# Chunk-selected attention with a gated projection: half-batch units for all heads, one fp32 transpose of keys and queries, and scores of a head pair in row tiles

## Chip, cores, metric

The kernel runs on one core of one Trainium2 chip. The metric is the device time of one execution in microseconds. Each kernel was run several times and compared with runs of the kernel before on the same chip.

## The reference, cut to what matters

Four batches, 8 heads, 768 positions, head size 64. Keys fall into 24 chunks of 32. For each query and chunk an upper bound of the score is computed from the chunk's minimum and maximum; each query keeps its six best chunks, and causal attention runs over those. The result (3072 rows of 512) goes through a gated projection with inner size 1536.

```python
k_min, k_max = k_chunks.min(axis=3), k_chunks.max(axis=3)        # 24 chunks of 32 keys
ub = sum over d of max(q * k_min, q * k_max)                     # bound per query and chunk
top_chunks = argsort(where(causal_chunk, ub, -1e9))[..., -6:]
scores = q @ k.T / 8, masked to the chosen chunks and to j <= i
attn = softmax(scores); x = attn @ v                             # (4, 768, 8*64)
out = (sigmoid(x @ w_gate) * (x @ w_val)) @ w_out                # 3072 x 512
```

## The kernel before

Work goes in 8 groups, each four heads of one batch over all 768 positions. The keys and queries of a head are turned so that head size lies on the partitions, in fp16, 64 rows; under them lie 32 more rows, which for the keys hold a fixed pattern (minus 60000 at the positions of chunk c in row c) and for the queries hold 1 where chunk c was *not* chosen. One matmul with 96 rows then gives score plus mask.

```python
def chunk_bounds(g):                       # kc: a second copy of the keys, one chunk per partition
    kv = d["kc"].rearrange("p s d -> p d s")
    nc.vector.tensor_reduce(kmm[:, 0:64], kv, AX.X, ALU.max)
    nc.vector.tensor_reduce(kmm[:, 64:128], kv, AX.X, ALU.min, negate=True)
...
def score(g, h, x):
    hk, hq = headK[4 * (g % 2) + h], headQ[4 * (g % 2) + h]      # both [96, 768]
    ...
    for (jb, i0, w) in banks[x]:
        nc.tensor.matmul(ps[:, o:o + w], hk[:, 128 * jb:128 * jb + 128], hq[:, i0:i0 + w],
                         start=True, stop=True)
        o += w
    nc.scalar.activation(at[:, b0:b0 + n], ps, AF.Exp, scale=scale)
...
for g in range(NG):                        # the projections of batch b run beside batch b + 1
    if g % 2 == 0 and g > 0:
        ffn = ffn_tasks(g // 2 - 1)
```

The chunk bounds are fp32 matmuls that write 32 output partitions each, so the four heads of a group use four column strips of the array at once. The projections of one batch (`ffn_gv`, `ffn_out`) are interleaved with the attention of the next batch.

The softmax here doesn't subtract the row's maximum and nothing guards it: scores larger than these inputs give would overflow.

## Time and profile before

| | before |
|---|---|
| time, median (4 runs) | 394.27 us |
| span of the profiled run | 393.6 us |
| TensorE matmul busy | 320.2 us (81%) |
| VectorE / ScalarE / GpSimd busy | 230.0 / 204.6 / 73.5 us |
| projections, third gate block starts | 114.1 us |
| TensorE idle between matmuls, whole span | 61.4 us |

From the page of the kernel before come busy time, the slices (each digit is the busy tenth of one fortieth of the span, 9 is 90% or more), and the granted TensorE clock in tenths (9 is full here, 5 is half):

```profile
span 393.6 us, 6906 instructions
...
PE 320.2 (81%) x2696; PEld 197.2 (50%) x2696; DVE 230.0 (58%) x486; ACT 204.6 (52%) x393; POOL 73.5 (19%) x77
...
PE   1071549287598999799979998799999999999996
...
PEclk9996557856969999999999999999999999999999
DMA  9999999297920964433615010002000100100102
```

The first quarter differs from the rest: TensorE is idle for nearly half of it (54 of 114 us in the table below) and often at half clock, while the DMA engines are full for most of it. After slice 12 TensorE hardly rests. The table of windows of the kernel before says the same in numbers (length of the window, busy time and instruction count of each engine, granted clock, DMA share, GB/s):

```profile
core 0: us, PE busy (x) PEld busy (x) DVE busy (x) ACT busy (x) POOL busy (x), PEclk, DMA share, GB/s
0.00:114.00 114.00, 59.58 (x509) 39.52 (x510) 77.07 (x156) 49.78 (x90) 36.34 (x43) 0.76 1.02 185
190.00:231.00 41.00, 36.95 (x337) 22.84 (x336) 27.52 (x57) 25.24 (x49) 7.88 (x7) 1.00 0.32 78
```

In the first quarter the chain of waits of the kernel before (start, length, what) goes through loads and the chunk reductions, not through TensorE:

```profile
0.81 5.91 DMA kc_151<-in_k_dram
6.74 3.59 DVE kmm_209 L140
10.33 3.50 DVE kmm_209 L141
...
39.69 11.32 DMA k_177<-in_k_dram
51.16 1.35 POOL k_1_349 L132
```

This is the timeline of TensorE in the kernel before around the chunk bounds (start, length, engine, line, operation, operands):

```profile
210.28 0.32 PE L287 MATMUL v_0_7_2464<-xT_1_1617,wv_146 128*128 128x384 f16 x1
210.44 0.33 PE L287 MATMUL v_0_7_2464<-xT_2_2033,wv_146 128*128 128x384 f16 x1
210.60 0.33 PE L287 MATMUL v_0_7_2464<-xT_3_2194,wv_146 128*128 128x384 f16 x1
210.86 0.46 PE L169 MATMUL ubT_2446<-qcat_0_2281,kcat_142 128*32 128x320 f32 x1
...
211.71 0.43 PE L169 MATMUL ubT_2446<-qcat_3_2386,kcat_142 128*32 128x320 f32 x1
212.07 0.34 PE L281 MATMUL g_0_8_2471<-xT_0_1456,wg_145 128*128 128x384 f16 x1
```

A matmul's length in the record (0.33 us for 384 columns) is not what it costs in a dense stream; that is the step to the next start, here 0.16 us (0.42 ns per column). Between the last full-array matmul (210.60) and the first one on a 32-column strip (210.86) the step is 0.26: 0.1 us more than streaming. On the way back it is 0.36 us where the passes among themselves step by 0.27.

### The profile page before, as it was taken

What the parts mean: (1) busy time and instruction counts of PE and PEld (TensorE: products, weight loads), DVE (VectorE), ACT (ScalarE), POOL (GpSimd) and SP (SyncE); (2) the same over time, 40 slices, a digit from 0 to 9 for tenths busy, and PEclk for the clock granted to TensorE, in tenths of its full rate; (3) what the DMA queues carried; (4) which work ended last, traced back from release to release, by engine and by line L of the source; (5) the groups of instructions that cost most, each with busy time, mean ns of one, the idle gap of its engine ahead of it and who ended that gap; (6) DMA issues with size and microseconds to landing.
All of it is one profiled execution on the core that took longest, in us unless ns stands there. A gap on an engine that the chain in (4) does not pass through costs nothing.

```text
span 393.6 us, 6906 instructions
## 1 busy us (share of the span) xinstructions
PE 320.2 (81%) x2696; PEld 197.2 (50%) x2696; DVE 230.0 (58%) x486; ACT 204.6 (52%) x393; POOL 73.5 (19%) x77
## 2 busy tenths in 40 slices
PE   1071549287598999799979998799999999999996
PEld 0040335164464656455645555465666566565552
DVE  4947629967949745855596658664556544142230
ACT  1150446266576548555556656655876466332331
POOL 4504143232312051003300230011101001000000
PEclk9996557856969999999999999999999999999999
DMA  9999999297920964433615010002000100100102
GB/s 181 217 214 214 208 212 195 66 217 148 214 62 15 226 156 108 101 62 86 155 42 120 28 55 0 2 2 80 2 2 27 55 2 1 55 27 28 54 2 80
DMA packets 84400, 36.62 MB, mean 93 GB/s; under 512 B 75920, under 2 KB 80528, under 8 KB 83600
## 3 DMA queue, kind: packets, MB, share of 16 engines
q1 hardware_dynamic: 79616, 31.47, 37.3%
q0 software_dynamic: 4752, 4.72, 7.2%
q8 instruction: 21, 0.34, 0.4%
q14 instruction: 11, 0.09, 0.1%
HBM read 34.60 MB, written 6.29 MB: 104 GB/s over the span
## 4 chain that ended last, share of the span: by engine, by line
PE 58%; DVE 17%; ACT 8%; issue 6%; SPq 5%; DMA 4%; POOL 1%; ACTq 0%; DVEq 0%; POOLq 0%
SPq L125 5%; DMA k_177<-in_k_dram 3%; DMA kc_151<-in_k_dram 2%; DVE kmm_1096 L140 1%; DVE kmm_209 L140 1%; DVE kmm_721 L141 1%; DVE kmm_1096 L141 1%; DVE kmm_209 L141 1%; PE o_0_0_2626 L296 1%; PE o_0_0_3781 L296 1%; PE o_384_0_3203 L296 1%; PE o_384_0_2048 L296 1%; PE o_0_0_1471 L296 1%; PE o_384_2_4783 L296 1%; PE o_384_1_4298 L296 1%
## 5 line engine op out<-in xcount | busy, mean ns | idle before, releaser
L287 PEld LDWEIGHTS <-wv_146 128*128 128x128 f16 x384 | 37.9, 99 | 28.3 <-issue 4.2
L281 PEld LDWEIGHTS <-wg_145 128*128 128x128 f16 x384 | 35.7, 99 | 23.2 <-issue 6.7
L153 PE MATMUL qT_0_212<-ident_103,q_148 128*128 128x128 f32 x5 | 1.3, 426 | 8.4 <-DMA q_148<-in_q_dram 8.4
L243 PEld LDWEIGHTS <-hk_123 96*128 96x128 f16 x48 | 4.8, 122 | 3.8 <-issue 2.9
L153 PE MATMUL qT_1_227<-ident_103,q_148 128*128 128x128 f32 x5 | 1.3, 427 | 5.9 <-DVE qcat_1_221 L160 5.9
L153 PE MATMUL qT_0_369<-ident_103,q_176 128*128 128x128 f32 x5 | 1.3, 426 | 5.8 <-DMA q_176<-in_q_dram 5.8
L140 DVE TENSOR_REDUCE kmm_1096<-kc_1044 96x64 f32<-96x2048 f32 x1 | 3.7, 3667 | 3.7 <-PE kct_756 L146 3.7
L272 PE MATMUL xps_1_671<-ident_108,xnat_400 128*128 128x128 f16 x6 | 0.8, 307 | 6.1 <-DVE xnat_400 L265 6.1
L140 DVE TENSOR_REDUCE kmm_209<-kc_151 96x64 f32<-96x2048 f32 x1 | 3.6, 3591 | 3.8 <-DMA kc_151<-in_k_dram 3.8
L272 PEld LDWEIGHTS <-xnat_400 128*128 128x128 f16 x24 | 2.1, 120 | 7.2 <-DVE xnat_400 L265 6.9
L243 PEld LDWEIGHTS <-hk_135 96*128 96x128 f16 x48 | 4.3, 109 | 2.4 <-issue 1.1
L290 DVE SCALAR_TENSOR_TENSOR hg_384_0_4595<-gate_384_0_4588,v_384_0_4590 128x384 f16<-128x384 f16 x1 | 0.6, 553 | 8.5 <-PE v_384_0_4590 L287 8.5
L243 PEld LDWEIGHTS <-hk_125 96*128 96x128 f16 x48 | 4.5, 110 | 1.9 <-issue 0.5
L193 PEld LDWEIGHTS <-ap_140 128*128 128x128 f16 x20 | 1.5, 106 | 7.7 <-DVE ap_140 L187 6.1
L264 DVE RECIPROCAL rz_0_423<-pv_0_401 128x6 f32<-128x6 f32 x1 | 0.2, 195 | 8.8 <-PE pv_0_401 L261 8.8
L193 PE MATMUL apT_316<-ident_108,ap_140 128*128 128x128 f16 x5 | 0.7, 309 | 5.7 <-DVE ap_140 L187 5.7
L243 PEld LDWEIGHTS <-hk_131 96*128 96x128 f16 x48 | 4.1, 107 | 2.3 <-issue 1.1
L243 PEld LDWEIGHTS <-hk_133 96*128 96x128 f16 x48 | 4.3, 108 | 1.8 <-issue 0.2
L153 PEld LDWEIGHTS qT_0_212<-ident_103,q_148 128*128 128x128 f32 x5 | 0.9, 220 | 8.3 <-issue 8.3
L140 DVE TENSOR_REDUCE kmm_359<-kc_179 96x64 f32<-96x2048 f32 x1 | 3.6, 3597 | 2.4 <-DMA kc_179<-in_k_dram 2.4
L261 PE MATMUL pv_0_401<-v_141,att_0_335 128*128 128x65 f16 x21 | 1.3, 244 | 4.5 <-POOL att_0_335 L249 4.5
L243 PEld LDWEIGHTS <-hk_127 96*128 96x128 f16 x48 | 4.2, 106 | 1.6 <-issue 0.2
(2400 smaller groups left out, 1201.9 us busy)
## 6 DMA issues: line engine op xcount, KB each, us to landing
wg_145<-in_moe_w_gate_dram POOLq DMA_DIRECT2D x3, 512.0 KB, 9.8
wv_146<-in_moe_w_val_dram POOLq DMA_DIRECT2D x3, 512.0 KB, 7.7
wo_147<-in_moe_w_out_dram POOLq DMA_DIRECT2D x3, 512.0 KB, 12.9
kc_151<-in_k_dram SPq DMA_DIRECT2D x1, 768.0 KB, 5.9
q_148<-in_q_dram SPq DMA_DIRECT2D x4, 192.0 KB, 6.6
k_149<-in_k_dram SPq DMA_DIRECT2D x4, 192.0 KB, 6.5
v_150<-in_v_dram SPq DMA_DIRECT2D x4, 192.0 KB, 7.3
kc_179<-in_k_dram SPq DMA_DIRECT2D x1, 768.0 KB, 17.0
```

The costliest lines, as they stand in the source:

```text
L125: nc.sync.dma_start(d[n][:, :, h, :], src[b, h0 + h].rearrange("(sb p) d -> p sb d", p=128))
L140: nc.vector.tensor_reduce(kmm[:, 0:64], kv, AX.X, ALU.max)
L141: nc.vector.tensor_reduce(kmm[:, 64:128], kv, AX.X, ALU.min, negate=True)
L153: nc.tensor.transpose(ps[:, 128 * i:128 * i + 128], d["q"][:, i + 1, 2 * pr:2 * pr + 2, :].rearrange("p h d -> p (h d)"), ident32)
L193: nc.tensor.transpose(ps[:, 128 * i:128 * i + 128], apt[g % 2][:, i, :, :].rearrange("p h c -> p (h c)"), ident16)
L243: nc.tensor.matmul(ps[:, o:o + w], hk[:, 128 * jb:128 * jb + 128], hq[:, i0:i0 + w], start=True, stop=True)
L261: nc.tensor.matmul(ps[:, ib, :], at[:, c:c + 128], v16s[g % 2][:, jb, h, :], start=(jb == 0), stop=(jb == ib))
L272: nc.tensor.transpose(ps[:, 128 * ib:128 * ib + 128], xnat[b][:, ib, 128 * c:128 * c + 128], ident16)
L281: nc.tensor.matmul(gp, wg16[:, c, 128 * fb:128 * fb + 128], xT[(b, c)][:, t0:t0 + TCH], start=(c == 0), stop=(c == 3))
L287: nc.tensor.matmul(vp, wv16[:, c, 128 * fb:128 * fb + 128], xT[(b, c)][:, t0:t0 + TCH], start=(c == 0), stop=(c == 3))
L290: nc.vector.scalar_tensor_tensor(hg, gate, 1.0, vp, ALU.add, ALU.mult)
L296: nc.tensor.matmul(op, hgl[(b, t0, fc)][:, 128 * tb:128 * tb + 128], wo16[:, fc, :], start=(fc == 0), stop=(fc == NFB - 1))
```

## The change

The intent: start the projections earlier by working in units of half a batch (384 queries, all 8 heads); load the keys once; transpose keys and queries once in fp32 and take from that PSUM tile both the fp16 copy and, for the keys, chunk maximum and minimum; and, instead of stacking 64 feature rows and 32 mask rows, issue them as separate matmuls, two heads at a time, each in its own rows of the array, so that a head pair would run at once. The diff, cut to its core:

```diff
-    def score(g, h, x):
-        hk, hq = headK[4 * (g % 2) + h], headQ[4 * (g % 2) + h]
...
-        for (jb, i0, w) in banks[x]:
-            nc.tensor.matmul(ps[:, o:o + w], hk[:, 128 * jb:128 * jb + 128], hq[:, i0:i0 + w],
-                             start=True, stop=True)
+    def score(u, heads, x):                      # heads: a pair
...
+        for (jb, i0, w) in u.banks[x]:
+            i = i0 - T * u.half
+            plain = i0 + w <= 128
+            if not plain:
+                for h in heads:
+                    r = 32 * (h % 4)             # 32 rows: the mask
+                    nc.tensor.matmul(ps[h][:, o:o + w], epat[r:r + 32, 128 * jb:128 * jb + 128],
+                                     u.mask[r:r + 32, h // 4, i:i + w], start=True, stop=False)
+            for h in heads:
+                r = 64 * (h % 2)                 # 64 rows: the keys
+                nc.tensor.matmul(ps[h][:, o:o + w], k16[u.b][r:r + 64, h // 2, 128 * jb:128 * jb + 128],
+                                 u.q16[r:r + 64, h // 2, i:i + w], start=plain, stop=True)
+            o += w
...
+    def keys_t(u, p, pool):
+        for x in range(HB):
+            nc.tensor.transpose(ps[:, 128 * x:128 * x + 128], ..., ident32)      # fp32, two heads
+        for e, op in enumerate((ALU.max, ALU.min)):
+            nc.vector.tensor_reduce(out=kmx[u.b % 2][:, p, e, c0:c0 + T // CH], in_=pv, op=op, axis=AX.X)
+        nc.scalar.copy(k16[u.b][:, p, u.rows], ps)
...
+    def bounds(u):
+        for e in range(2):                       # maximum with relu(q), then minimum with min(q, 0)
+            for i in range(4):
+                for j in range(2):
+                    c = i ^ j
+                    h = 4 * j + c
+                    r = 64 * (h % 2)
+                    nc.tensor.matmul(ps[j][32 * c:32 * c + 32, 0:n], kmx[u.b % 2][r:r + 64, h // 2, e, :],
+                                     u.qs[r:r + 64, h // 2, e, s0:T], start=(e == 0), stop=(e == 1))
...
+    for i, u in enumerate(units):                # 8 units: batch b, half a or b
+        a = attend_tasks(u, prep)                # prep: of the next unit
+        merge(a, prev)                           # prev: projections of the unit before
+        prev = ffn_tasks(u)
```

Counted on the program order of TensorE, the *tiling mode* (full array, 64-row tiles, 32-row tiles, 32-column strips) changes 16 times in the kernel before and 656 times in the changed one.

## The prediction

> **What bounds the kernel now.** Two regimes. From 114 us to the end the granted clock is 1.0 (one dip, 165 to 169 us) and TensorE is the limit: in the table of windows it is busy 37.8 to 38.5 of each 41 to 42 us, and it runs alone in the last 46 us. The projections cannot shrink: matmuls 128x384 start every 162 ns and 128x512 every 216 ns (timeline), 768 and 288 of them, 187 us. The rest of TensorE's work, by start-to-start times at full clock, is about 102 us: scores 39, values 20.5, q transposes 9, f16 transposes 11, bounds 10, others 12. Sum 290, span 393.6. The difference is mostly the first 114 us: TensorE starts at 8.4 us, is busy 53 of the first 107 us, and has the half clock for 55 us of that stretch; the DMA engines are full (about 210 GB/s) until 70 us; the projections cannot run steadily before all heads of batch 0 are done (single matmuls at 68 to 112 us, steady from 114 us). There the chain of waits goes through loads and VectorE's chunk reductions (3.6 us each).
>
> **What the change removes and adds.**
> - Loads: the second copy of the keys (6.3 MB of 34.6) goes.
> - VectorE: reductions 58 us become 64 from PSUM of 384 elements at an estimated 0.55 us (384-element PSUM operations take 0.55), 35 us; mask rows and feature copies (33 us) become 14; sign split 26 becomes 16. Estimate 195 us instead of 230. ScalarE stays near 205. Neither bounds the steady part.
> - TensorE: 192 fp32 transposes at 109 ns (21 us) replace 80 plus 192 f16 ones (20 us). Bounds about equal. Scores: keys 18 us if two row tiles really overlap, mask matmuls 17 more: 35 to 37 against 39. So 290 us again, before switching.
> - New: scores alternate between 32-row and 64-row tiles. In program order the tiling mode changes 656 times instead of 16. The Trainium skill, "TensorEngine Tiling (Array Packing)", Key Properties, says that a change of mode drains the engine. The trace agrees for the bounds' column tiles: 95 ns is lost on entering and on leaving (365 ns instead of 270). If row tiles cost that too, 60 us are added; I count half, 30.
> - Half-batch units let projections begin after one low half: loads of two units plus competing weights, estimated steady at 46 us instead of 114.
>
> **On the critical path.** At 46 us about 15 us of attention work is done. Remaining: 188 + 85, some 17 us idle (6%, as between 180 and 340 us before), 0 to 56 us of switches: 336 to 392. The head gains some 65 us; switches give part back.
>
> **Predicted: 363 us, 8 in 10 between 338 and 394.** Faster by over 2%: 0.80; within 2%: 0.13; slower: 0.07.
>
> **What would show it.** Steady projections from 40 to 55 us; half clock only before about 60 us; TensorE over 90% busy afterwards; the two heads' key matmuls starting within some 10 ns of each other; at each change between mask and key matmuls a start-to-start time over the streaming time: its size times 656 is the bill.
>
> **What would make it wrong.** Row tiles that do not overlap, or switches above 95 ns because weight loads cannot run ahead over them (slower, 400 or more); free switches (about 340); three score buffers shared by pairs and values starving TensorE behind the exponentials; weights and unit loads sharing the DMA so that the second unit comes after 50 us.

## More of the kernel before

A verdict of faster or slower needs 2%.

## The result and the profile after

The changed kernel takes 429.69 us (median of 4 runs, 426.47 to 431.17) against 394.27: slower, ratio 1.089 (interval 1.083 to 1.096). Ratios are the mean time of one kernel's runs over that of the other's of the same rounds, so they are not quite the ratio of the medians quoted. Executions over 1.5% slower than the fastest of the same kernel are left out of the means. The prediction, 363 us with a range of 338 to 394, was wrong.

The lines of the page of the changed kernel that answer to those above:

```profile
span 427.7 us, 8087 instructions
...
PE 399.7 (93%) x3280; PEld 220.9 (52%) x3280; DVE 174.1 (41%) x527; ACT 189.5 (44%) x401; POOL 55.8 (13%) x94
...
PE   0278979999999999999999999999999999999996
...
PEclk9995686999999996999999996999999999899999
DMA  9999998663193320303103320000100010000102
```

The first quarter has filled up as intended, and VectorE has shed 56 us. But TensorE is now recorded as busy for 80 us more. The windows of the changed kernel:

```profile
core 0: us, PE busy (x) PEld busy (x) DVE busy (x) ACT busy (x) POOL busy (x), PEclk, DMA share, GB/s
0.00:74.00 74.00, 49.63 (x327) 25.63 (x328) 30.42 (x106) 21.87 (x48) 21.39 (x35) 0.79 1.08 192
190.00:231.00 41.00, 41.00 (x371) 23.78 (x369) 18.54 (x58) 20.14 (x43) 5.84 (x8) 1.00 0.25 59
```

From 74 us on, where the third gate block starts (114.1 us before), TensorE is not idle for 0.2 us in total, so every nanosecond added to it is added to the time. The timeline of TensorE in the changed kernel shows what is added:

```profile
265.25 0.22 PE L244 MATMUL sc_2b_3_3368<-mask_2b,epat 32*128 32x128 f16 x1
265.26 0.23 PE L244 MATMUL sc_2b_3_3369<-mask_2b,epat 32*128 32x128 f16 x1
265.41 0.23 PE L248 MATMUL sc_2b_3_3368<-q_2b,k_2_2014 64*128 64x128 f16 x1
265.42 0.23 PE L248 MATMUL sc_2b_3_3369<-q_2b,k_2_2014 64*128 64x128 f16 x1
265.57 0.28 PE L244 MATMUL sc_2b_3_3368<-mask_2b,epat 32*128 32x256 f16 x1
265.58 0.28 PE L244 MATMUL sc_2b_3_3369<-mask_2b,epat 32*128 32x256 f16 x1
265.79 0.28 PE L248 MATMUL sc_2b_3_3368<-q_2b,k_2_2014 64*128 64x256 f16 x1
265.79 0.28 PE L248 MATMUL sc_2b_3_3369<-q_2b,k_2_2014 64*128 64x256 f16 x1
```

The two heads of a pair start within 10 ns of each other, so the row tiles do overlap. But the step from the mask pair to the key pair is 0.16 us for 128 columns, which stream in 0.053, and 0.21 us for 256, which stream in 0.107. Each change between 32-row and 64-row tiles costs about 0.105 us, whatever the number of columns.

What these 0.105 us consist of is less clear. The weight loads of the same matmuls (PEld), and below them two of run b1_one_mode (an experiment further down), where the mode does not change:

```profile
265.41 0.10 PEld L248 LDWEIGHTS <-k_2_2014 64*128 64x128 f16 x2
265.57 0.09 PEld L244 LDWEIGHTS <-epat 32*128 32x128 f16 x2
...
240.53 0.10 PEld L252 LDWEIGHTS <-k 64*128 64x128 f16 x2
240.59 0.10 PEld L248 LDWEIGHTS <-epad 64*128 64x128 f16 x2
```

At a change the load begins with its own matmul (265.41 and 265.57, the starts above); without a change it begins one matmul earlier (240.53 for the matmul of 240.58). Over the whole trace at full clock, loads at a change begin 4 ns ahead of their matmul (median of 560), others 54 ns. At a change, then, no load runs ahead, and one load is recorded as 0.09 to 0.10 us, nearly the price of the change. Whether that price is the waiting for the array to empty or the uncovered load, no run here separates: every change in these kernels comes with new weights.

I added up the steps between matmul starts over the whole trace. Idle time is apart; where the tiling mode changes, what a step has over its streaming time (0.417 ns per column, fp32 twice that, halved clock doubled) goes to "changes of mode"; what the half clock adds to streaming is apart too; what remains goes to the kind of matmul. "Start and end" is the time before the first matmul and after the last one's end. In us:

| TensorE's account | before | after | difference |
|---|---|---|---|
| projections | 191.7 | 189.1 | -2.6 |
| scores | 40.1 | 42.3 | +2.2 |
| values | 20.6 | 20.6 | 0.0 |
| transposes | 37.3 | 39.1 | +1.8 |
| chunk bounds | 9.8 | 21.1 | +11.3 |
| **changes of tiling mode** | 1.8 | 69.2 | **+67.4** |
| half clock, extra | 19.0 | 18.3 | -0.7 |
| idle | 61.4 | 20.4 | **-41.0** |
| start and end | 11.9 | 7.6 | -4.3 |
| span | 393.6 | 427.7 | +34.1 |

The gain the change was made for is there (45 us of idle time and start). It is more than spent by 656 changes of mode, with a median excess of 105 ns each, and by the bounds.

### The profile page after: what moved, and what is told of

Its sections match the earlier page's. It is cut to its first block, busy times and chain, and to the rows that moved or that the text cites. A ratio compares the mean times of both kernels' runs of the same rounds, so it can differ in the third digit from the quotient of the medians.

```text
span 427.7 us, 8087 instructions
## 1 busy us (share of the span) xinstructions
PE 399.7 (93%) x3280; PEld 220.9 (52%) x3280; DVE 174.1 (41%) x527; ACT 189.5 (44%) x401; POOL 55.8 (13%) x94
## 4 chain that ended last, share of the span: by engine, by line
PE 88%; SPq 6%; DMA 4%; DVE 1%; issue 0%; ACT 0%
SPq L99 6%; DMA q_0b<-in_q_dram 4%; PE o_1b_3178 L306 1%; PE o_1b_3128 L306 1%; PE o_3a_5109 L306 1%; PE o_2b_4479 L306 1%; PE o_2b_4429 L306 1%; PE o_2a_3823 L306 1%; PE o_1a_2510 L306 1%; PE o_0b_1865 L306 1%; PE o_0b_1815 L306 1%; PE o_0a_1359 L306 1%; PE o_0a_1197 L306 1%; PE o_3a_5058 L306 1%; PE o_2a_3985 L306 1%; PE o_1a_2672 L306 1%
## 5 line engine op out<-in xcount | busy, mean ns | idle before, releaser
L297 PEld LDWEIGHTS <-wv_157 128*128 128x128 f16 x384 | 38.6, 100 | 25.9 <-issue 3.0
L291 PEld LDWEIGHTS <-wg_156 128*128 128x128 f16 x384 | 32.4, 99 | 22.7 <-issue 4.9
L244 PEld LDWEIGHTS <-epat 32*128 32x128 f16 x448 | 24.7, 92 | 33.9 <-issue 20.5
L248 PEld LDWEIGHTS <-k_0_159 64*128 64x128 f16 x120 | 7.1, 95 | 9.7 <-issue 4.7
L158 PE MATMUL kT_0a_160<-ident_118,k_0a 128*128 128x128 f32 x3 | 1.4, 467 | 9.6 <-DMA k_0a<-in_k_dram 9.6
L248 PEld LDWEIGHTS <-k_3_3327 64*128 64x128 f16 x120 | 6.6, 92 | 7.1 <-issue 2.0
L248 PEld LDWEIGHTS <-k_2_2014 64*128 64x128 f16 x120 | 6.5, 93 | 7.2 <-issue 2.4
L248 PEld LDWEIGHTS <-k_1_701 64*128 64x128 f16 x120 | 6.5, 93 | 7.1 <-issue 2.4
L172 PE MATMUL qT_0a_190<-ident_118,q_0a 128*128 128x128 f32 x3 | 1.4, 457 | 8.2 <-DMA q_0a<-in_q_dram 8.2
L192 PE MATMUL ubT_0b_505<-qs_0b,kmx_144 64*32 64x384 f32 x16 | 4.1, 660 | 0.0
L192 PE MATMUL ubT_0b_506<-qs_0b,kmx_144 64*32 64x384 f32 x16 | 4.0, 660 | 0.0
L163 DVE TENSOR_REDUCE kmx_144<-kT_0a_160 128x12 f32<-128x384 f32 x2 | 1.0, 552 | 7.4 <-PE kT_0a_160 L158 7.4
L111 POOL TENSOR_SCALAR_AFFINE_SELECT epat<-epat 32x768 f16<-32x768 f16 x4 | 4.0, 991 | 0.2
L225 PEld LDWEIGHTS <-ap_145 128*128 128x128 f16 x20 | 1.3, 97 | 5.2 <-DVE ap_145 L217 5.2
L151 POOL CAST v_146<-v_0a 128x1536 f16<-128x1536 f32 x1 | 1.5, 1462 | 16.0 <-DMA v_0a<-in_v_dram 16.0
L192 PE MATMUL ubT_2b_3069<-qs_2b,kmx_144 64*32 64x384 f32 x16 | 3.2, 487 | 0.0
```

The lines of the kernel that those rows point to most:

```text
L111: nc.gpsimd.affine_select(out=epat[32 * h:32 * h + 32], in_=epat[32 * h:32 * h + 32], compare_op=ALU.not_equal, fill=NEG, base=0, pattern= ...
L151: nc.gpsimd.tensor_copy(v16s[u.b % 2][:, u.qa:u.qb, :, 0:D], u.v)
L158: nc.tensor.transpose(ps[:, 128 * x:128 * x + 128], u.k[:, x, 2 * p:2 * p + 2, :].rearrange("p h d -> p (h d)"), ident32)
L172: nc.tensor.transpose(ps[:, 128 * x:128 * x + 128], u.q[:, x, 2 * p:2 * p + 2, :].rearrange("p h d -> p (h d)"), ident32)
L192: nc.tensor.matmul(ps[j][32 * c:32 * c + 32, 0:n], kmx[u.b % 2][r:r + 64, h // 2, e, :], u.qs[r:r + 64, h // 2, e, s0:T], start=(e == 0), ...
L244: nc.tensor.matmul(ps[h][:, o:o + w], epat[r:r + 32, 128 * jb:128 * jb + 128], u.mask[r:r + 32, h // 4, i:i + w], start=True, stop=False)
```

## Experiments

My first theory (theory 1): each change of tiling mode costs a fixed 105 ns of a saturated TensorE. Rival theory 2: the mode is not to blame; small row-tile matmuls are slow in any order, because two weight loads per pair do not hide, or because the tiles do not overlap. Rival theory 3: not the scores but the half-batch units or the fp32 preparation cost the time. The runs a1, b1, c1 and e1 shared one chip and one set of runs of the kernel before (392.85 us), the runs d1, c2, g1 and f1 another (393.46); across the sets, compare ratios rather than medians. All eight gave correct results.

### a1_grouped: the same matmuls in another order

```diff
-        for (jb, i0, w) in u.banks[x]:            # per block: masks of the pair, keys of the pair
+        for keys in (False, True):                # per bank: all masks, then all keys
+            for (jb, i0, w) in u.banks[x]:
+                ...   masks only if not keys, start=first; keys only if keys, start=False
```

> Only the order of the score matmuls changes: in each score bank all mask matmuls go first, then all key matmuls (only the first mask matmul of a bank clears it). Same matmuls, same weight loads, same tiles. Changes of tile mode in program order fall from 656 to 348. Theory 1 (each change of tile mode costs a fixed 105 ns on a saturated TensorE, whatever the clock): 308 x 0.105 = 32 us less than the changed kernel, so about 396 us. Rival theory 2 (row tiles are slow because two weight loads per pair of small matmuls cannot hide, or because row tiles do not really overlap): no change, 425 to 430 us.

Measured: 394.15 us (391.07 to 397.37; the last counts as slow and is not in the ratio), ratio to before 0.999. The matmuls are the same, 308 changes of mode are gone, and 36 us went: theory 1 holds, theory 2 would have seen no change. In this trace the changes of mode add up to 34.4 us (69.2 in the changed kernel). The match is not quite as clean as it looks: the granted clock also rose from 0.944 to 0.969, which is 24 us at half clock instead of 48, while scores, bounds and other terms of the account grew by some 4 us. A detail makes the edit possible: only the first mask matmul of a bank carries the start flag. The Trainium skill, "PSUM — Partial Sum Buffer", The four PSUM rules, says that the flag clears the marks of the whole bank (in the partitions that the matmul writes), so a second one would spoil an open sum; the correct result of this run, with a single flag per bank, fits that, but a second flag was not tried.

### b1_one_mode: masks in the keys' mode

The mask matmuls take 64 rows (two heads' masks) against weights that are zero for the other head, so masks and keys use the same 64-row tiles.

```diff
+    epad = consts.tile([128, 2, S], F16, tag="epad")        # zero, but for one head's pattern
-                    r = 32 * (h % 4)
-                    nc.tensor.matmul(ps[h][:, o:o + w], epat[r:r + 32, ...], u.mask[r:r + 32, ...], ...)
+                    r = 64 * (h % 2)
+                    nc.tensor.matmul(ps[h][:, o:o + w], epad[r:r + 64, (h % 4) // 2, ...], u.mask[r:r + 64, ...], ...)
```

(The order of the heads in the bounds changes with it, still on four tiles.)

> The mask matmuls read 64 rows instead of 32, the other head's 32 rows meeting zero weights, so that they run in the same 64-row tiles as the keys; number of matmuls, weight loads and streamed columns unchanged. Changes of tile mode fall from 656 to 220. Theory 1: 436 x 0.105 = 46 us less than the changed kernel, about 383 us. Theory 2: no change, 425 to 430 us.

Measured: 385.12 us (384.13 to 386.23), ratio 0.979 (interval 0.975 to 0.983; against the limit of 2% that counts as unclear, against the changed kernel's 1.089 it is plain). The timeline of TensorE in this run (x2 is the two heads):

```profile
240.52 0.23 PE L248 MATMUL sc_2b<-mask_2b,epad 64*128 64x128 f16 x2
240.58 0.22 PE L252 MATMUL sc_2b<-q_2b,k 64*128 64x128 f16 x2
240.64 0.22 PE L248 MATMUL sc_2b<-mask_2b,epad 64*128 64x128 f16 x2
240.70 0.22 PE L252 MATMUL sc_2b<-q_2b,k 64*128 64x128 f16 x2
...
240.92 0.22 PE L252 MATMUL sc_2b<-q_2b,k 64*128 64x128 f16 x2
241.07 0.82 PE L295 MATMUL g_2a<-xT_2a,wg 128*128 128x384 f16 x4
```

A pair of 128-column matmuls now steps by 0.06 us, weight loads and all, where the changed kernel needs 0.16 for the same columns. Only entering from the full array and going back to it (240.92 to 241.07) still cost 0.1 us extra each; these are the 220 changes that remain. So theory 2 falls as a property of row tiles: two 64-row tiles do run in the time of one, and within a mode their weight loads hide. At a change they do not, as shown above. The Trainium skill, "TensorE: Matmul & The Clock Gate", Part 3, says that matmuls on different row groups run at once, starting a few ns apart; this trace agrees (the two of a pair start 3 ns apart, median).

### c1_full_rows: no row tiles in the scores

```diff
-            for h in heads: ...                   # masks in 32-row tiles, keys in 64-row tiles
+        for h in heads:                           # 64 key rows and 32 pattern rows stacked, as before
+            for (jb, i0, w) in u.banks[x]:
+                nc.tensor.matmul(ps[h][:, o:o + w], headK[u.b % 2][h][:, 128 * jb:128 * jb + 128],
+                                 headQ[u.half][h][:, i:i + w], start=True, stop=True)
```

The copies out of PSUM go to one tile per head again (two copies of 64 rows instead of one of 128; four mask copies instead of one).

> The changed kernel without row tiles in the scores: keys and mask pattern again stacked to 96 rows per head, one matmul per block in the full array; half-batch units, fp32 transposes, chunk max and min from PSUM all kept; 16 more copies per unit on ScalarE and VectorE. Changes of mode 22 instead of 656. Theory 1: 67 us less in switches, streaming about equal (39 us against 36): about 360 us, clearly faster than before (394). Rival theory 3 (the half-batch units or the fp32 transposes cost the time): stays above 400 us.

Measured: 366.88 us (366.26 to 368.83), ratio 0.934. Theory 3 falls: units, single load, fp32 transposes and reductions from PSUM are worth 26 us as soon as the row tiles are gone. The scores cost the same 42.3 us in TensorE's account as in the changed kernel, and the changes of mode 2.2 us. It is 7 us more than expected; 30.0 us of idle time appear where the changed kernel had 20.4. The chain of waits of this run names where:

```profile
26.70 24.05 DMA v_0b<-in_v_dram
50.87 1.46 POOL v L157
52.33 0.48 POOL att_0a L251
52.85 0.24 PE pv_0a L265
```

TensorE waits for the diagonal select of a head of unit 0a, which sits on GpSimd's queue behind the cast of the values of unit 0b, which land only at 50.9 us.

The four kernels give time against number of changes: 656 changes 429.7 us, 348 changes 394.2, 220 changes 385.1, 22 changes 366.9. From end to end that is 63 us for 634 changes, 99 ns each. This is a net figure: between the two ends the time at half clock also fell (granted clock 0.944 and 0.981, that is 48 and 14 us) and idle time grew by 10 us. Whether the changes bring on the half clock was not tested.

### d1_before_row_tiles: the kernel before with row tiles alone

```diff
-    def score(g, h, x):           # [96, S] per head, one matmul per block
+    def score(g, pr, x):          # per pair: masks[g % 2][r:r + 32], pairK / pairQ[r:r + 64], as in the changed kernel
```

> The kernel before with one part of the change alone: scores of a head pair in row tiles (64-row key tiles, 32-row mask tiles, in the order of the changed kernel); units, loads, chunk reductions and prep as before, feature and mask copies fewer. Changes of tile mode about 574 instead of 16. Theory 1: 558 x 0.105 = 59 us of TensorE time, of which that in the first quarter is partly hidden because TensorE has idle time there: 435 to 450 us. Rival theory 3 (units and prep cost the time, row tiles are harmless): within 2% of before, 385 to 400 us.

Measured: 441.35 us (437.78 to 442.46), ratio 1.118. The excess at changes of mode adds up to 60.5 us in this trace and the time grows by 48: part of it falls in idle time of the first quarter (idle between matmuls 40.4 us; in the kernel before, counted the same way with the first start, 69.8), and on the other side the granted clock was lower, 0.899 (0.93 to 0.957 in the runs of the kernel before of this set). The trace has 581 changes, 574 were expected. The row tiles alone make the old kernel slower than the changed one. (This variant also needs fewer copies, walks through heads in pairs and keeps five attention tiles instead of three, so it is not quite one edit.)

### e1_bounds8: the other term

In the changed kernel's bounds, head `4*j + c` with `c = i ^ j` lies in rows `64*(c % 2)` and columns `32*c` for both `j`: eight heads on only four tiles.

```diff
-                    c = i ^ j
-                    h = 4 * j + c
+                    c = i
+                    h = 4 * j + (c ^ j)          # rows 64*((c + j) % 2): eight distinct tiles
```

(The rows of the masks in the scores follow the new places; the number of changes stays 656.)

> Only the place of the heads in the chunk bounds changes, so that the 8 heads use 8 distinct tiles of the array; in the changed kernel both groups of four heads use the same 4 tiles. If the bounds' 21 us on TensorE come from two groups taking turns on four tiles, this removes about 9 us: about 420 us. If 64-row tiles of 32 columns do not overlap further, no change (427 to 431 us).

Measured: 424.00 us (423.51 to 425.55), ratio 1.078 against 1.089: 5.7 us off the median, some 4 us by the ratios, less than the 9 expected. From the first bound matmul to the next other matmul a high unit took 3.10 us in the changed kernel and takes 1.81 here; a low one 2.25 and 1.81. So the shared tiles cost time, but eight tiles are not twice as fast as four, and a low unit with 256 columns takes as long as a high one with 384. That is not the doing of the tiles alone: with the same eight tiles in g1_cast_last a low unit takes 1.23 us and a high one 1.97. Why was not pursued.

### c2_full_rows_bounds8: both repairs

```diff
+   the edits of c1_full_rows and of e1_bounds8 together
```

> The variant without row tiles in the scores (367 us) plus the bounds on eight distinct tiles. The latter alone gave 6 us on the changed kernel (430 to 424); if the two add up: 361 us. If bounds are hidden once TensorE is less loaded: 366 us.

Measured: 363.66 us (362.57 to 364.06), ratio 0.923 against c1's 0.934. By the medians 3 us of e1's 6 remain; by the ratios, which allow for the two sets of runs, the step is 0.011 in both cases. So the runs do not show that the gain shrinks.

### g1_cast_last: GpSimd's queue

```diff
-        r.append((0.0, lambda: cast_v(u)))                       # in the next unit's preparation
+        a.append((0.0, lambda i=i: cast_v(units[i + 1])))        # at the end of this unit's list
```

> As the variant without row tiles and with eight-tile bounds, but GpSimd's cast of a unit's values is put at the end of the previous unit's list instead of ahead of that unit's last diagonal selects. In the variant the trace shows GpSimd waiting 18 us for the values of unit 0b (landed at 50.9 us) with four selects of unit 0a behind it, TensorE idle 7.7 us. If that queue order costs the time: 4 to 8 us less than without it, about 355. If the load is what counts and the next unit is late anyway: no change, 360 to 362.

Measured: 361.00 us (360.78 to 361.24), ratio 0.917. A gain of 2.7 us against c2_full_rows_bounds8, less than expected, and the third gate block starts at 74.7 us, no earlier (73.6). But this run does not test what it was meant to. The edit changed the order in the program, and not the order on GpSimd at the place in question:

```profile
51.51 1.46 POOL L157 CAST v<-v_0b 128x1536 f16<-128x1536 f32 x1 [19.06 <-DMA v_0b<-in_v_dram]
52.92 1.94 POOL L251 TENSOR_SCALAR_AFFINE_SELECT att_0a<-att_0a 128x384 f16<-128x384 f16 x4
```

The cast of unit 0b still waits 19 us for its values, with four selects of unit 0a behind it, and TensorE's wait for a select grew from 8.9 to 10.1 us. So the queue order stays untested, and what gained the 2.7 us is open.

### f1_weights_late: who shares the DMA engines at the start

```diff
     for i in range(3):
+        for w in (wg16, wv16):                   # waits for the queries of unit 0b; the load overwrites it
+            nc.gpsimd.tensor_copy(w[0:1, 0:1, 512 * i:512 * i + 1], units[1].q[0:1, 2:3, 0:1, 0:1]...)
         load_w(i)
```

(The same for `wo16`; the rest is g1_cast_last.)

> As the variant with the late cast, and in addition the nine loads of the projection weights start only after the queries of unit 0b have landed (a one-element copy into each weight tile waits for them, and the load overwrites it). In the changed kernel these loads share the DMA engines with the first two units: queries of 0b landed at 42.5 us instead of the estimated 20 to 25. If that sharing is why steady projections began at 65 us instead of the predicted 46: they begin at 48 to 55 and the time falls by 6 to 12 us against the late cast alone, about 345 to 350. If not: no change or worse, because the weights come later.

Measured: 350.36 us (349.19 to 351.35), ratio 0.890: 10.6 us less than with the late cast alone, and 11% less than the kernel before. The loads of unit 0b's values now land 5.1 us after their issue instead of 23.3 (medians of three). So the weights did hold the first units' loads back. The run changes more than the sharing of the DMA engines, though: here the four selects do run before the cast, and the issues of the weight loads have moved on GpSimd's queue.

```profile
39.91 1.94 POOL L251 TENSOR_SCALAR_AFFINE_SELECT att_0a<-att_0a 128x384 f16<-128x384 f16 x4
41.80 1.46 POOL L157 CAST v<-v_0b 128x1536 f16<-128x1536 f32 x1
```

TensorE's wait for a select falls from 10.1 to 1.9 us, most of the gain. With the values landed by 25 us the cast would not have waited in the old order either, so the sharing is the likelier part; neither was run alone.

The size of the gain was expected, the place only in part: the third gate block starts at 62.7 us, not at 48 to 55. The copies that hold the weights back sit on GpSimd behind one select each of four heads, the last of them begun after 29.8 us, so the first weight load is issued at 31.8 us. The windows of this run:

```profile
core 0: us, PE busy (x) PEld busy (x) DVE busy (x) ACT busy (x) POOL busy (x), PEclk, DMA share, GB/s
0.00:63.00 63.00, 40.11 (x298) 26.35 (x299) 41.91 (x137) 30.59 (x67) 30.22 (x54) 0.89 1.23 200
190.00:231.00 41.00, 40.35 (x383) 25.67 (x380) 27.87 (x82) 26.63 (x60) 4.06 (x8) 1.00 0.15 40
```

TensorE is still busy 40.35 of 41 us in the middle, so what is left to win lies in the first 63 us and in TensorE's work itself. This kernel beats both.

## Why the prediction was wrong, point by point

- **The limit of the steady part: right.** TensorE bounds it; the 56 us that VectorE lost bought nothing there.
- **Work without switching "290 us again": nearly right.** Scores 42.3 against 40.1 and transposes 39.1 against 37.3 in the account. "Bounds about equal" was wrong by 11.3 us: I took 64-row tiles with 32 columns to mean eight at once, and the index arithmetic puts both groups of four heads on the same four tiles. It was there to be read in the diff. Even on eight tiles (e1_bounds8) they cost 14.6 us, counted the same way.
- **The failed step: "I count half, 30."** The Trainium skill ("TensorEngine Tiling (Array Packing)", Key Properties) said that a change of mode drains the engine, the trace of the kernel before showed 95 ns for column strips in both directions, and the program order gave 656 changes. I had all three factors and then halved the product, on the hope that row tiles might be cheaper. They cost 105 ns; the term measured 69.2 us. The mechanism was right, the term was mis-sized by 39 us. a1_grouped, b1_one_mode and c1_full_rows show that it is the changes and not the row tiles as such; what a change spends its time on is open (emptying the array, or the uncovered weight load). The prediction had named the second as a danger, weight loads that cannot run ahead over a switch, and the trace shows that they do not.
- **"The head gains some 65 us": too much.** Idle time, start and half clock together fell by 46 us; the third gate block starts at 74 us and not at 46. The estimate let the first two units load at nearly the full DMA rate; the weights took their share, the queries of 0b were awaited until 42.5 us, and TensorE ran at half clock from 31.7 to 48.8 us. Later weights were worth 10.6 us in f1_weights_late, a new order on GpSimd's queue included; that switches stretch the head further was not tested apart.
- **"Some 17 us idle" afterwards: 0.1 us.** A saturated TensorE has no idle time left to hide the switches in. The two errors partly cancel.
- **"Free switches (about 340)"**: nearest to it is c2_full_rows_bounds8 with 363.66 us; its third gate block starts at 73.6 us and not at 46, which is more than the rest of the distance.

The upper end of my sum, 392, already had nearly the full switching cost (56 us). It failed because head and bounds failed with it, all three in the same direction.

## What to carry to other kernels

Count the changes of tiling mode in the program order, multiply by the cost that a trace shows for one, and do not discount the product; on a saturated TensorE it is paid in full. If row tiles are used, keep to long runs of one mode: grouping the matmuls by mode cut the time to 394 us here, padding the smaller ones with zero rows into the mode of the larger ones to 385. Neither made row tiles pay: without them it was 367, and apart from the changes the scores cost TensorE the same 42.3 us either way. When half of a change hides a gain and half a loss, as here, take the halves apart: without its row tiles the same change was 7% faster than before, and with small repairs of the start and the bounds 11%.

## What the Trainium skill lacked or had wrong

- "TensorEngine Tiling (Array Packing)", Key Properties, says that changing the mode drains TensorE but gives no cost. Here: 105 ns median between 32-row and 64-row tiles and 98 to 105 ns between full array and row tiles at full clock; between 32-row and 64-row tiles at half clock 108 to 111 ns, so there nearly a fixed time; but 140 ns from the full array into row tiles at half clock (13 changes). The 656 changes cost 69.2 us of 427.7. In these traces the weight load at a change begins with its matmul and not ahead of it.
- "TensorE: Matmul & The Clock Gate", Part 3, recommends row tiles for small contractions without a word on mixing modes. Here two 64-row tiles of 128 columns step by 0.06 us in one mode and by 0.16 us when 32-row tiles stand between.
- The same page, Part 1, ties the half clock to idle TensorE. In the changed kernel the granted clock fell to half at 161.4 and at 257.0 us, for 6.8 us each (and at 362.8 us for 3.4), in stretches where the profile shows TensorE busy 40.0 of 40 us; in the six variants of the changed kernel with 348 changes of mode or fewer it does not happen after 75 us but at the very end. The recorded busy time bridges the 0.1 us of each change, so this does not contradict the page; the cause was not tested.
- None of the pages that I read gives a time for tiles of 64 rows and 32 columns in fp32: in e1_bounds8 eight distinct tiles took 1.81 us where four took 3.10 (384 columns) and 2.25 (256 columns); in g1_cast_last eight took 1.97 and 1.23.
